# S4 convolution beside a gated FFN on one core: where the second half of the decay exponentials is made

## The chip, the core and the metric

The kernel runs on one core of one Trainium2 chip. The time is device microseconds of one execution, and the median of several executions is quoted. Five engines work side by side: TensorE (PE, with its weight loads PEld), VectorE (DVE), ScalarE (ACT), GpSimd (POOL) and SyncE (SP, which here only issues DMAs).

## The reference, cut to what matters

The reference normalises the input, runs an S4 convolution and a gated FFN on it, adds both to the input, and returns that output with the gradients of twelve inputs. L = 2048 positions, D = 576 channels, N = 128 states per channel, F = 4608.

```python
xn = layernorm(u)
# S4: a long convolution with a kernel K made from the parameters
dt = exp(log_dt)[:, None]
logdA = dt * (A_re + 1j * A_im)                    # [D, N]
P = exp(logdA[:, :, None] * arange(L))             # [D, N, L]
K = einsum("dn,dnl,dn->dl", C, P, dt * B).real     # [D, L]
y = irfft(rfft(pad(xn)) * rfft(pad(K)))[:L] + xn * Dskip
# FFN
gate, up = xn @ W_gate, xn @ W_up
h = relu(gate) * up
out = u + y + h @ W_down
# and the gradients of all of this for a given grad_out
```

The part that the change is about is the real factor of P: exp(dt * A_re * l). It is made at 40 exponents l for each channel and state (16 small steps, 8 steps of 256, 16 steps of 16), and products of these give all 2048.

## The kernel before, in words

Two generators make the program. `Ffn.gen` emits the FFN: 12 chunks of 384 hidden columns; in each chunk four groups of 512 positions go through `a_unit` (three products into PSUM, gating on ACT and DVE) and `outdx` (output and input gradient), and after the last group come the weight gradients (`dw_down`, `dw_gu`, `dw_left`), which are long series of matmuls with few evictions. `S4.gen` emits the convolution in the stages below. Both yield estimated microseconds. The main function advances `S4.gen` by 0.9 units (`PACE`) for each unit that the FFN has yielded. The framework then puts each engine's instructions into one queue per engine, in roughly this order, but ahead of it where it expects an instruction to be ready earlier; the profile shows such moves of some microseconds.

`S4.gen` works on two halves of the channels, 288 each:

- `p1(hf)` transforms the input and the output gradient, multiplies the spectra and makes dk, the gradient of K. It has three sections, with a gap of units ahead of each.
- `params` loads the parameters, makes `pw` (four rows of products per channel), and makes the decay exponentials in 36 steps of 16 channels, named `ex_step`: DVE multiplies `pw` by the 40 exponents into a tile of 128 x 640 fp32, ACT takes Exp in place, and SP stores it to the DRAM tensor `ex_dram` (320 KB). The tile, `exs`, has five rotating buffers (pool `par_ex`).
- `p2(hf)` makes K from the parameters, 16 channels at a time (18 times for a half): it loads a tile `ex` back from `ex_dram` (two buffers, pool `k_ex`), makes angles in `xa` and `W` (one buffer each, pool `k_x`; `W` is two tiles of 128 x 640 side by side; lines L838 to L843), and multiplies. `sums` and `turn` use the result on TensorE. At its end `param_grads` uses `xa` and `W` once more.
- `p3(hf)` transforms K and finishes the convolution of that half.

`both(a, wa, b, wb)` weaves two generators so that their yields stand in the ratio wa to wb. The order is

```python
both(p1(0), 68, params, 45)
both(p2(0), 320, p1(1), 60)
both(p2(1), 320, p3(0), 58)
p3(1)
```

Added up, the yields are 82 units for `p1(0)`, 42 for `params`, 382 for each `p2`, 61 for `p1(1)`, 49 for `p3(0)` and 59 for `p3(1)`. In the last chunk of the FFN, `outdx` takes the results of both `p3` into its sums; whatever is left of `S4.gen` is emitted before that.

DVE and ACT evictions from PSUM are shared out by `Balance.copy`, which keeps a running estimate of the work of both engines and takes the less loaded one.

Of the kernel before, what the change touches and what calls it, by code (L numbers as in the profile page):

```python
# [2 lines left out]

# [7 lines left out]
F32 = mybir.dt.float32  # L11
ACT = mybir.ActivationFunctionType
ALU = mybir.AluOpType
AX = mybir.AxisListType
P = 128
# [5 lines left out]
L, D, F, N = 2048, 576, 4608, 128  # L21
ST = 16
DH = D // 2
# [8 lines left out]
SX = 16  # L32
NE = 40
# [3 lines left out]
W1, W2, W3 = 60.0, 400.0, 58.0  # L37
# [58 lines left out]
def iota(nc, ap, pattern, base, mult):  # L96
    nc.gpsimd.iota(ap, pattern=pattern, base=base, channel_multiplier=mult, allow_small_or_imprecise_dtypes=True)
# [378 lines left out]
class S4:  # L476
# [85 lines left out]
    def params(self, pw):  # L562

        g, nc, bal = self.g, self.g.nc, self.g.bal
        v = nc.vector
        with ExitStack() as c:
            pool = self.pool(c, "par_raw", 1)
            exp_ = self.pool(c, "par_ex", 5)
            raw = pool.tile([P, 6, D], BF16, name="raw")
            nc.sync.dma_start(raw[:], self.par_in[:])  # L570
            ldt = pool.tile([P, D], BF16, name="ldt")
            nc.sync.dma_start(ldt[:], self.log_dt.rearrange("(o d) -> o d", o=1).to_broadcast([P, D]))
            yield 1.0
            dt = pool.tile([P, D], F32, name="dtf")
            nc.scalar.activation(dt[:], ldt[:], ACT.Exp)
            nc.sync.dma_start(self.dt_dram[:], dt[:])
            Ar, Ai, Br, Bi, Cr, Ci = (raw[:, i, :] for i in range(6))
            v.tensor_tensor(pw[:, 0, :], Ar, dt[:], op=ALU.mult)
            bal.add(d=0.7, a=0.7)
            yield 1.0  # L580

            def ex_step(i):
                shp = [P, SX, NE]
                ex = exp_.tile(shp, F32, name="exs")
                v.tensor_tensor(ex[:], pw[:, 0, i * SX:(i + 1) * SX].unsqueeze(2).to_broadcast(shp), self.ev[:].unsqueeze(1).to_broadcast(shp), op=ALU.mult)
                nc.scalar.activation(ex[:], ex[:], ACT.Exp)
                nc.sync.dma_start(self.ex_dram[:, i], ex[:])
                bal.add(d=0.75, a=0.65)

            for i in range(0, 8):  # L590
                ex_step(i)
                yield 1.0
            p1 = pool.tile([P, D], F32, name="p1")
            p2 = pool.tile([P, D], F32, name="p2")
            v.scalar_tensor_tensor(pw[:, 1, :], Ai, 1.0 / TWO_PI, dt[:], op0=ALU.mult, op1=ALU.mult)
            for j, (y1, y2, op) in enumerate(((Br, Bi, ALU.subtract), (Bi, Br, ALU.add))):
                v.tensor_tensor(p1[:], Cr, y1, op=ALU.mult)
                v.tensor_tensor(p2[:], Ci, y2, op=ALU.mult)
                v.tensor_tensor(p1[:], p1[:], p2[:], op=op)
                v.tensor_tensor(pw[:, 2 + j, :], p1[:], dt[:], op=ALU.mult)  # L600
                bal.add(d=2.6)
                yield 2.0
            for i in range(8, D // SX):
                ex_step(i)
                yield 1.0

    def dft(self, pool, dram):

        def load(m):
            S = pool.tile([P, 2, 2, P], BF16, name="Sx")  # L610
            self.g.nc.sync.dma_start(S[:], dram[:, 2 * m:2 * m + 2])
            return S
        return load
# [394 lines left out]
    def gen(self):  # L1008
        g, nc = self.g, self.g.nc
        self.make_dft16()  # L1010
        yield 1.0
        yield from self.make_dft128()
        with ExitStack() as cp:
            kp = self.pool(cp, "s4_par", 1)
            pw = kp.tile([P, 4, D], F32, name="pw")
            self.ev = kp.tile([P, NE], F32, name="ev")
            self.ones = kp.tile([P, 1], F32, name="ones")
            nc.vector.memset(self.ones[:], 1.0)
            iota(nc, self.ev[:, 0:16], [[1, 16]], 0, 0)
            iota(nc, self.ev[:, 16:24], [[256, 8]], 0, 0)  # L1020
            iota(nc, self.ev[:, 24:40], [[16, 16]], 0, 0)
            yield from self.both(self.p1(0, 4, 10.0), 68.0, self.params(pw), 45.0)
            with ExitStack() as c:
                pools = self.p2_pools(c)
                yield from self.both(self.p2(0, pools, pw), 0.8 * W2, self.p1(1, 2, 3.0), W1)
                yield from self.both(self.p2(1, pools, pw), 0.8 * W2, self.p3(0, 2, 3.0), W3)
            yield from self.p3(1, 4, 8.0)

class Final:
# [216 lines left out]
```

## Time and profile before

| | us |
|---|---|
| median of 3 runs | 1824.65 (1823.95 to 1829.02) |
| the profiled execution, its time | 1821.82 |
| its span | 1820.1 |
| TensorE busy | 1732.4 (95%) |
| VectorE busy | 1352.4 (74%) |
| ScalarE busy | 1188.5 (65%) |
| first and last start of an exponential step on DVE | 102.3 and 215.8 |
| first start of L838 in p2(0) | 229.6 |
| first start of L838 in p2(1) | 892.6 |
| last store of p3(1) | about 1609 |

The profile is one execution. A line of it names the line of the kernel, the engine, the operation and its tiles, and in square brackets how long the engine stood idle just before, and who ended that. A busy TensorE is not TensorE at its peak, since matmuls overlap. The granted clock is 1.00 almost everywhere.

### The profile page before, as it was taken

The page shows a single profiled execution, that of the slowest core. Times are in us where ns is not written, and L with a number is a line of the kernel's source. Part 1 is how long each engine was busy: PE and PEld are TensorE (multiplying, and loading weights), DVE is VectorE, ACT ScalarE, POOL GpSimd, SP SyncE. Part 2 cuts the span into 40 slices and gives each one's busy share as a digit, 9 for nine tenths or more (in the row PEclk, how much of TensorE's full clock was granted, in tenths as well). Part 3 has the DMA queues.
Part 4 walks back from the last instruction along what each step waited for, and adds up shares of the span by engine and source line. Part 5 has one row for each costly group of instructions (what it writes and reads, how often), then busy time and mean ns, then how long its engine had stood idle before and what let it go on. Part 6 is the DMA issues. An engine that isn't in the chain of part 4 may idle for free. (4 is left out here: it accounts for less than half of the span.)

```text
span 1820.1 us, 42158 instructions
## 1 busy us (share of the span) xinstructions
PE 1732.4 (95%) x16303; PEld 1182.6 (65%) x16449; DVE 1352.4 (74%) x3175; ACT 1188.5 (65%) x2716; POOL 204.6 (11%) x246
## 2 busy tenths in 40 slices
PE   7998989999999999999999999999999998999998
PEld 5664557667666666766766766766676775466776
DVE  7575885786898788687787888899888865952551
ACT  5875865786588478577478657747857837852551
POOL 0200012111012012102101101101111100010000
PEclk9999999999999999999999999999999999999999
DMA  8789999668557666776866856865665689884883
GB/s 287 261 313 320 304 290 276 191 176 230 178 127 191 197 183 140 238 187 125 238 171 162 227 166 138 206 193 133 166 182 142 133 230 273 252 238 131 264 247 97
DMA packets 239004, 373.30 MB, mean 205 GB/s; under 512 B 49490, under 2 KB 153428, under 8 KB 237268
## 3 DMA queue, kind: packets, MB, share of 16 engines
q1 hardware_dynamic: 212836, 304.09, 51.3%
q0 software_dynamic: 24384, 51.92, 19.1%
q10 hardware_dynamic: 1584, 14.60, 2.2%
q8 instruction: 128, 2.10, 0.5%
q14 instruction: 72, 0.59, 0.1%
HBM read 233.10 MB, written 137.43 MB: 204 GB/s over the span
## 5 line engine op out<-in xcount | busy, mean ns | idle before, releaser
L68 ACT CAST osx<-ps_mm 128x288 bf16<-128x288 f32 x682 | 262.1, 420 | 61.9 <-PE ps_mm L301 59.2
L314 POOL DMA_DIRECT2D acc_dram<-osx x160 | 139.2, 876 | 1016.6 <-ACT osx L68 680.5
L301 PE MATMUL ps_mm<-wf,dgT 128*128 128x288 bf16 x1152 | 207.0, 286 | 8.5 <-ACT osx L68 5.3
L355 PEld LDWEIGHTS <-rows 128*128 128x128 bf16 x1536 | 146.6, 98 | 95.0 <-issue 3.1
L301 PE MATMUL ps_mm<-wf,duT 128*128 128x288 bf16 x1152 | 205.8, 286 | 0.0
L301 PE MATMUL ps_mm<-wf,hT 128*128 128x288 bf16 x1152 | 183.8, 287 | 7.9 <-DVE hT L256 4.3
L244 PE MATMUL ps_mm<-gT,wd_160 128*128 128x512 bf16 x694 | 177.3, 382 | 7.2 <-ACT obd L68 5.3
L244 PE MATMUL ps_mm<-xT,wd_159 128*128 128x512 bf16 x711 | 180.8, 381 | 0.8 <-ACT obw L68 0.3
L244 PE MATMUL ps_mm<-xT,wd_158 128*128 128x512 bf16 x595 | 168.8, 379 | 7.9 <-issue 1.0
L254 DVE SCALAR_TENSOR_TENSOR upm<-rg,ps_mm 128x512 bf16<-128x512 bf16 x144 | 98.2, 682 | 102.0 <-PE ps_mm L244 80.2
L339 PE MATMUL ps_mm<-rows,hN 128*128 128x144 bf16 x2304 | 156.7, 226 | 0.0
L339 PEld LDWEIGHTS <-hN 128*128 128x128 bf16 x2304 | 147.0, 98 | 3.4 <-issue 1.2
L355 PE MATMUL ps_mm<-duN,rows 128*128 128x384 bf16 x768 | 137.9, 326 | 0.0
L355 PE MATMUL ps_mm<-dgN,rows 128*128 128x384 bf16 x768 | 136.9, 327 | 0.0
L68 ACT CAST obw<-ps_mm 128x384 bf16<-128x384 f32 x102 | 48.5, 477 | 133.7 <-PE ps_mm L355 98.9
L301 PEld LDWEIGHTS <-dgT 128*128 128x128 bf16 x1152 | 106.0, 97 | 40.5 <-issue 15.1
L301 PEld LDWEIGHTS <-duT 128*128 128x128 bf16 x1152 | 112.1, 98 | 29.1 <-DVE duT L264 0.2
L301 PEld LDWEIGHTS <-hT 128*128 128x128 bf16 x1152 | 104.5, 98 | 37.1 <-issue 8.2
L68 ACT CAST dhb<-ps_mm 128x512 bf16<-128x512 f32 x141 | 83.8, 594 | 64.5 <-PE ps_mm L244 60.8
L930 DVE TENSOR_REDUCE Sm<-pr 128x8 f32<-128x256 f32 x288 | 119.1, 414 | 3.5
L252 ACT ACTIVATE rg<-ps_mm 128x512 bf16<-128x512 f32 x144 | 87.0, 604 | 51.1 <-PE ps_mm L244 47.4
L244 PEld LDWEIGHTS <-wd_159 128*128 128x128 bf16 x720 | 65.4, 98 | 62.6 <-issue 3.6
(2516 smaller groups left out, 3516.1 us busy)
## 6 DMA issues: line engine op xcount, KB each, us to landing
acc_dram<-osx POOLq DMA_DIRECT2D x176, 288.0 KB, 4.8
gT<-in_gT_dram SPq DMA_DIRECT2D x48, 640.0 KB, 6.4
xT<-xT_dram SPq DMA_DIRECT2D x44, 640.0 KB, 6.0
rows<-in_gq_dram SPq DMA_DIRECT2D x48, 576.0 KB, 4.6
wf<-in_Wf_dram ACTq DMA_DIRECT2D x11, 1296.0 KB, 9.7
ex_dram<-exs SPq DMA_DIRECT2D x36, 320.0 KB, 3.7
ex<-ex_dram SPq DMA_DIRECT2D x36, 320.0 KB, 3.6
out_dram<-obw SPq DMA_DIRECT2D x96, 96.0 KB, 2.7
```

Of the source, the lines that this page charges most:

```text
L68: self.nc.scalar.copy(out, in_)
L244: nc.tensor.matmul(ps[:], lhsT=w[:, k, fs], rhs=rhs[:, k, :], start=(k == 0), stop=(k == NK - 1))
L252: nc.scalar.activation(rg[:], ps_g[:], ACT.Relu)
L254: nc.vector.scalar_tensor_tensor(upm[:], rg[:], 0.0, ps_u[:], op0=ALU.is_gt, op1=ALU.mult)
L301: nc.tensor.matmul(ps[:, cs], lhsT=lt, rhs=rh, start=(i == 0), stop=(i == len(mms) - 1))
L314: nc.gpsimd.dma_start(g.acc_dram[:, t, :, :], o[:], accum_op=ALU.add)
L339: nc.tensor.matmul(ps[:, ft * 144:(ft + 1) * 144], lhsT=self.hN[:, st, ft * P:(ft + 1) * P], rhs=gq[:, st, :], start=(st == 0), stop=(st = ...
L355: nc.tensor.matmul(ps[:, :Fc], lhsT=xs[:, st, 0:P], rhs=src[:, st, :], start=(st == 0), stop=(st == ST - 1))
L930: nc.vector.tensor_reduce(out=Sm[:, vi, s0 + dd:s0 + dd + DG, :], in_=pr[:], op=ALU.add, axis=AX.X)
```

## The change

`params` makes only the 18 exponential steps of the first half of the channels (8 of them before the products of `pw`, 10 after). The other 18 are made by a new generator, `late_ex`, which runs right after `p2(0)` and its `param_grads`, ahead of `p2(1)` and inside the same weave with `p3(0)`. It takes its five buffers from the pools of `p2`: the two halves of `W`, `xa`, and the two `ex` tiles. Each of its steps yields 1.2 units where a step in `params` yielded 1.0. Step, tiles and `ex_dram` keep their shapes. The five buffers `exs` of `params` stay as they are.

```diff
-            for i in range(0, 8):
-                ex_step(i)
+            for i in range(0, 8):
+                self.ex_step(i, exp_.tile([P, SX, NE], F32, name="exs")[:], pw)
                 yield 1.0
...
-            for i in range(8, D // SX):
-                ex_step(i)
+            for i in range(8, DH // SX):
+                self.ex_step(i, exp_.tile([P, SX, NE], F32, name="exs")[:], pw)
                 yield 1.0
+
+    def ex_step(self, i, ex, pw):
+        nc = self.g.nc
+        shp = [P, SX, NE]
+        nc.vector.tensor_tensor(ex, pw[:, 0, i * SX:(i + 1) * SX].unsqueeze(2).to_broadcast(shp), self.ev[:].unsqueeze(1).to_broadcast(shp), op=ALU.mult)
+        nc.scalar.activation(ex, ex, ACT.Exp)
+        nc.sync.dma_start(self.ex_dram[:, i], ex)
+        self.g.bal.add(d=0.75, a=0.65)
+
+    def late_ex(self, pools, pw):
+        exp_, xp = pools[3], pools[4]
+        todo = list(range(DH // SX, D // SX))
+        while todo:
+            W = xp.tile([P, 2, SX, NE], F32, name="W")
+            bufs = [W[:, 0], W[:, 1], xp.tile([P, SX, NE], F32, name="xa")[:]] + [exp_.tile([P, SX, NE], F32, name="ex")[:] for _ in range(2)]
+            for b, i in zip(bufs, todo[:5]):
+                self.ex_step(i, b, pw)
+                yield 1.2
+            todo = todo[5:]
...
-                yield from self.both(self.p2(1, pools, pw), 0.8 * W2, self.p3(0, 2, 3.0), W3)
+                yield from self.both(chain(self.late_ex(pools, pw), self.p2(1, pools, pw)), 0.8 * W2, self.p3(0, 2, 3.0), W3)
```

More of the change, by code (lines that the diff above doesn't have):

```diff
@@ L2 @@
 from contextlib import ExitStack
+from itertools import chain
 import concourse.bass as bass
@@ L580, in params @@
             yield 1.0
[L582 to L588, printed above, removed]
             for i in range(0, 8):
-                ex_step(i)
+                self.ex_step(i, exp_.tile([P, SX, NE], F32, name="exs")[:], pw)
                 yield 1.0
```

## The prediction

> **What bounds the kernel now.** The busy table comes first:
>
> ```profile
> PE 1732.4 (95%) x16303; PEld 1182.6 (65%) x16449; DVE 1352.4 (74%) x3175; ACT 1188.5 (65%) x2716; POOL 204.6 (11%) x246
> ```
>
> TensorE is busy for 1732.4 of 1820.1 us. Its work does not change, so what moves the end is its 88 us of idle time. Next, the stages (columns: length, then busy time and instructions of each engine, granted clock, DMA share, GB/s):
>
> ```profile
> 158.00:230.00 72.00, 68.09 (x493) 37.39 (x497) 61.62 (x162) 57.58 (x142) 4.28 (x5) 1.00 0.94 309
> 230.00:300.00 70.00, 64.80 (x575) 45.30 (x579) 54.16 (x133) 47.28 (x110) 14.55 (x15) 0.98 0.98 286
> 300.00:850.00 550.00, 534.75 (x5310) 367.95 (x5358) 428.85 (x939) 384.19 (x874) 71.71 (x75) 1.00 0.70 186
> 850.00:905.00 55.00, 54.68 (x584) 40.52 (x587) 41.01 (x90) 29.14 (x63) 8.66 (x10) 1.00 0.79 206
> 905.00:1476.00 571.00, 548.60 (x5592) 384.75 (x5637) 490.61 (x1115) 395.49 (x881) 74.21 (x78) 0.99 0.67 171
> ```
>
> From 158 to 230 us, where most exponentials are made, DVE, ACT and the DMA engines are all near full, yet TensorE loses only 72 - 68.1 = 3.9 us. Around 850 to 905, where the change puts half of them, TensorE loses 0.3 us. Third, the exponential tile (durations are min/median/max ns; below, what its engine waited for):
>
> ```profile
> L585 DVE TENSOR_TENSOR exs<-pw,ev x36: 815/819/827, 102.3 to 215.8; 128x640 f32<-128x640 f32 x36
> L586 ACT ACTIVATE exs<-exs x36: 726/739/867, 103.6 to 216.7; 128x640 f32<-128x640 f32 x36
> ...
>   DMA ex_dram<-exs: 14.7, 4
> ...
> DMA to landing us min/median/max: 2.3/3.7/7.0
> ```
>
> DVE stood four times, 14.7 us in all, because a buffer's store had not landed. The timelines of DVE and of TensorE show what that costs TensorE:
>
> ```profile
> 144.77 0.82 DVE L585 TENSOR_TENSOR exs<-pw,ev 128x640 f32<-128x640 f32 x1 [8.06 <-DMA ex_dram<-exs]
> 207.70 0.83 DVE L585 TENSOR_TENSOR exs<-pw,ev 128x640 f32<-128x640 f32 x1 [3.55 <-DMA ex_dram<-exs]
> ```
>
> ```profile
> 146.82 2.25 PE L244 MATMUL ps_mm<-gT,wd_160 128*128 128x512 bf16 x5 [5.28 <-ACT obd L68]
> 209.32 0.31 PE L645 MATMUL ps_s_3202<-b_ug,FM 128*64 128x288 bf16 x2 [1.89 <-DVE s_ug L62]
> ```
>
> The wait of 8.06 us held ACT's exponential, an eviction behind it and then TensorE for 5.28 us. The five matmuls after it took 2.25 us where 1.24 is usual: about 1 us more. The wait of 3.55 us cost 1.89 us, and 0.52 us at 212.2. Counting in the DVE timeline, the 18th step starts at 160.1 us: the first wait belongs to step 14, which stays; the second to step 34, which moves.
>
> [...]
>
> **The change part by part.** Pace first. The conv generator is advanced in units that its yields add up to. From L838's first start, 229.6 us, to its first in half 1, 892.6 us, lie 382 units of p2(0) and 61 of p1(1): 663/443, about 1.5 us a unit; between 160 and 230 it is about 1.4. Params shrinks from 42 units to 24, and 21.6 (18 x 1.2) appear before p2(1). So the first p2 starts 18 x 1.4 = 25 us earlier; the late stage, with 0.18 of p3(0) per unit, lasts 21.6 x 1.18 x 1.4 = 36 us, about 868 to 904; everything behind ends 3.6 units, about 5 us, later.
>
> *Early, removed.* 18 DVE steps x 0.819 = 14.7 us, 18 exponentials x 0.739 = 13.3 us of ACT, 18 stores x 320 KB = 5.9 MB of the window's 22.2 MB, 18 issues on SP (median 0.44 us, 8 us of SP). On TensorE the direct gain is the wait of step 34: 1.89 + 0.52 = 2.4 us.
>
> *Early, given back.* p1(0) is no longer diluted. Per unit of p1 params ran 45/68 = 0.66; the rest of p1(0) after params' 24th unit (24/0.66 = 36 of 82) follows back to back. In the 72 us window the engines did 61.6 + 57.6 = 119.2 us. It shrinks to 47; leave out 18 x 1.56 = 28 and 25 us of FFN work at some 0.37 us per us (9): 82 in 2 x 47 = 87%, against 119.2/144 = 83% before. DMA comes out alike: 22.2 - 5.9 - 1.9 = 14.4 MB in 47 us is 306 GB/s, against 309. So the stage is shorter, not emptier. I book 1 us of gain net: below the 2.4 saved, for the denser rest; bounds -7 (nearly all idle from 158 to 300, 3.9 + 5.2, goes) and +3.
>
> *Late, steps.* The same 14.7 us of DVE and 13.3 of ACT in 36 us, in a stage where both have room (41 and 29 of 55 us) and p2 makes no other demand: nothing on TensorE. If that cover went, DVE's 14.7 us would hold FFN evictions; at the rate above (5.28 of 8.06) up to 9.6. The stores are denser than before: 5.9 MB in 36 us is 164 GB/s on top of the stage's 206, together 370, above the 309 that the early window reached at share 0.94. So DMA is full there, and the chunk's rows, xT, gT and wd loads come later; TensorE lost 3.9/72 = 5% in the early window under such a load, which is 2 us of 36. A part of that is the waits priced next; for late loads alone I book +1 (0 to 4).
>
> *Late, new waits.* A step comes every 1.2 x 1.18 x 1.4 = 2.0 us. W's two halves are one buffer, so a new round waits for the store of the half written four steps before: 8 us. It needs 0.82 + 0.74 + 0.44 + 0.5 (hand-offs, my estimate) + 3.7 = 6.2 us, or 9.5 with the slowest landing: 0 to 1.5 us at three round starts, book 1 in all. The last turn is tighter: p2(1)'s L838 writes xa, which step 18 has just sent off, 2.0 us after it; 6.2 - 2.0 = 4.2 us of wait on DVE, where the kernel before went on at 892.61 at once. Behind it in DVE's queue stand FFN's L254 to L264 and copies, and TensorE waits for these. At 5.28/8.06, rounded down because this is the stage of long dw matmuls, +2 (0 to 5). ex stores wait on SP for an exponential, with rows, xT and gT loads behind them on that queue; these are issued ahead, and their lateness is in the 1 us above. The two ex tiles that p2(1) loads were sent off in step 15 at the latest and are free first.
>
> *Late, tables.* One more Exp stage between Sin stages: two loads x 1.28 = 2.6 us of ACT, book +0.5 (0 to 2.6[...]).
>
> *Shift.* From about 205 to 868 the conv work meets other FFN chunks, 25 us off, later 5 us off. TensorE loses 550 - 534.8 = 15 us in 300-850 and 571 - 548.6 = 22 in 905-1476, in stalls that depend on such meetings. Mean 0, -5 to +7.
>
> *Tail.* The final matmuls start at 1673.6 us, p3(1)'s last stores go out near 1609; 5 us later still leaves some 60. Nothing, whatever the sign.
>
> Sum: -1 + 1 + 1 + 2 + 0.5 = +3.5 us. The profiled execution (span 1820.1, time 1821.8) becomes 1825.3; it lies 2.8 below the median 1824.65, so the forecast is 1828.1.
>
> **Rivals.** *Slower: the wait comes back as the bound.* The late stage falls on FFN's change of chunk, where wd, wf, xT, gT and rows are loaded and the 40-slice DMA row of that stretch has long full parts. Should landings reach 7 us and more with the planned order behind reality, the rounds' starts cost what step 14 did: 5.28 + 1 = 6.3 us on TensorE for 8 us of DVE wait. It decides from landings above 5.5 us, where the 1.8 us of spare is used up. One such stall plus the turn at 5 and the tables at 2.6 gives 14, less the early 1: 1837.6; without the full stall, 1831.3. For it: two of 36 steps paid such waits early at DMA share 0.94, and the late stage asks for more bytes per us. Against: five buffers at a step per 2.0 us, and few evictions among the dw matmuls.
>
> *Faster: the early relief is real.* The congestion of 158-300 goes: -7, the late stage costs 1, 1818.6. For it: three resources near full there. Against: the densities above, and only 2.4 us that trace back to moved steps.
>
> *The change does nothing,* because the planner that writes the queues fills the hole with p1 steps and TensorE never saw it: 1824.65, inside the first case.
>
> **How the numbers follow.** 0.3%, or 5.5 us, is about what a measurement of this kernel can tell from no change. Small net (likeliest, 1828.1, own range 1819.2 to 1830.1): 0.44. Slower, with the bad end of the shift: 0.41. Faster, with its good end: 0.15. The range 1819 to 1841 leaves out about a tenth at each end.
>
> **What would show it.** Right: 18 L585-type steps before 165 us and 18 near 865-905; first L838 near 205, first of half 1 near 904 after some 4 us of DVE waiting for a store; six table loads for four; the stall at 146.8 still there; final matmuls fed in time. Wrong: a TensorE idle above 3 us in 860-910 that traces back to ex_dram (slower rival), or idle in 158-300 down from 9 us to below 4 (faster rival). If neither holds and the time still moves by over 6 us, the shift was mis-sized.

## The result, and the profile after

| | before | after |
|---|---|---|
| median, us | 1824.74 | 1851.49 (1850.27 to 1854.88, 4 runs) |
| profiled execution, time / span, us | 1821.82 / 1820.1 | 1854.88 / 1853.2 |

The ratio of after to before is 1.0145, interval [1.0124, 1.0165]: slower by 26.5 us of 1824.7. The forecast was 1828.1, and its range ended at 1841.

The busy table of the profile page of after:

```profile
PE 1744.3 (94%) x16304; PEld 1185.9 (64%) x16449; DVE 1355.2 (73%) x3174; ACT 1195.3 (65%) x2721; POOL 205.3 (11%) x246
```

The same matmuls are busy 12 us longer in a span that is 33 us longer. The stages of after, in the windows that the prediction used (length; busy time and instructions of PE, PEld, DVE, ACT, POOL; granted clock; DMA share; GB/s):

```profile
158.00:230.00 72.00, 70.06 (x503) 36.38 (x508) 59.52 (x175) 54.12 (x139) 3.44 (x4) 1.00 0.91 288
230.00:300.00 70.00, 59.43 (x462) 40.28 (x467) 51.72 (x108) 43.09 (x101) 15.49 (x16) 0.90 0.79 203
300.00:850.00 550.00, 531.65 (x5331) 367.87 (x5375) 429.30 (x934) 381.89 (x861) 69.51 (x73) 1.00 0.70 187
850.00:905.00 55.00, 47.86 (x439) 34.13 (x441) 36.87 (x78) 34.23 (x76) 11.05 (x12) 0.94 0.76 182
905.00:1476.00 571.00, 538.94 (x5364) 372.94 (x5410) 479.95 (x1096) 387.37 (x856) 69.44 (x72) 0.99 0.67 171
```

From 158 to 230 us TensorE is busy 2 us longer than before, about the gain that the prediction had worked out there. From 230 to 300, where neither kernel makes exponentials, it is busy for 59.4 us where it was 64.8, does 462 matmuls instead of 575, and the clock is 0.90. From 850 to 905 it lost 6.8 us, and 9.7 more behind. In the window 230 to 300 DVE, ACT and the DMA engines are all less busy than before while TensorE idles more, so the early loss is not one of full engines.

The exponential steps of after, in the view of their line on DVE (min/median/max ns; first and last start; indented, what DVE waited for just before them, us and times). The line was L585 before and is L604 here:

```profile
L604 DVE TENSOR_TENSOR exs<-pw,ev x18: 814/821/826, 101.9 to 159.9; 128x640 f32<-128x640 f32 x18
...
L604 DVE TENSOR_TENSOR W<-pw,ev x8: 802/820/826, 889.3 to 921.6; 128x640 f32<-128x640 f32 x8
L604 DVE TENSOR_TENSOR ex<-pw,ev x6: 808/820/826, 796.5 to 845.3; 128x640 f32<-128x640 f32 x6
L604 DVE TENSOR_TENSOR xa<-pw,ev x4: 817/826/827, 886.7 to 923.3; 128x640 f32<-128x640 f32 x4
...
  DMA ex_dram<-W: 18.0, 3
...
  DMA ex_dram<-xa: 8.1, 3
  DMA ex_dram<-ex: 5.7, 2
```

The 18 early steps end at 160 us. The 18 late ones are not the rotation of five buffers that the code writes: the six steps in `ex` start 40 to 90 us ahead of the others, among the last turns of p2(0), because these two tiles came free earlier (`param_grads` still worked in W and xa until 886 us). What is left turns on W and xa alone. In the late stage DVE stood 18.0 + 8.1 + 5.7 = 31.8 us. Its timeline in the late stage (start, us, instructions; in brackets the idle time before and who ended it):

```profile
896.57 0.83 DVE L604 TENSOR_TENSOR xa<-pw,ev 128x640 f32<-128x640 f32 x1 [5.72 <-DMA ex_dram<-xa]
901.10 1.56 DVE L604 TENSOR_TENSOR W<-pw,ev 128x640 f32<-128x640 f32 x2 [3.70 <-DMA ex_dram<-W]
...
912.30 1.56 DVE L604 TENSOR_TENSOR W<-pw,ev 128x640 f32<-128x640 f32 x2 [7.37 <-DMA ex_dram<-W]
920.84 1.56 DVE L604 TENSOR_TENSOR W<-pw,ev 128x640 f32<-128x640 f32 x2 [6.98 <-DMA ex_dram<-W]
```

The stores themselves were slow here. For the 12 that left W and xa from 885 to 930 us, as far as the profile has their landing:

```profile
DMA to landing us min/median/max: 2.7/6.1/9.1
```

Those sent off between 889.8 and 903.6 us took 5.8 to 9.1 us, and the first three waits above end as such a store lands. From 885 to 905 us the DMA share is 0.97: the loads of the FFN's next chunk run beside them.

And what two of these waits did on ACT and on TensorE, from the timelines of these engines:

```profile
921.70 0.74 ACT L605 ACTIVATE W<-W 128x640 f32<-128x640 f32 x1 [5.73 <-DVE W L604]
922.35 0.50 ACT L69 CAST obd<-ps_mm 128x432 bf16<-128x432 f32 x1
```

```profile
898.51 0.88 PE L302 MATMUL ps_mm<-wf,dgT 128*128 128x288 bf16 x3 [3.26 <-ACT osx L69]
922.90 2.29 PE L245 MATMUL ps_mm<-gT,wd_160 128*128 128x512 bf16 x5 [5.60 <-ACT obd L69]
```

This is the chain of step 14 again: a store not landed, DVE waits, ACT's exponential waits for DVE, an eviction stands behind the exponential, TensorE waits for the eviction. The wait of 7.37 us that ended at 912.30 lay beside 168 dw matmuls in a row (902.78 to 914.22) and cost only 0.76 us.

The third place is early, where p2(0) and p1(1) start. TensorE's timeline there:

```profile
243.56 0.66 PE L698 MATMUL ps_s_3734<-bC_3678,Sx 128*128 128x288 bf16 x2 [4.64 <-DMA bC_3678<-C_dk_191]
270.62 0.88 PE L302 MATMUL ps_mm<-wf,dgT 128*128 128x288 bf16 x3 [4.01 <-ACT osx L69]
309.81 0.28 PE L642 MATMUL ps_s_4701<-sig,Sx 128*128 128x288 bf16 x1 [4.06 <-ACT fA_4657 L69]
```

None of the three touches an exponential. The first waits for a load of p1(0)'s last section, the second for an eviction behind a step of p2(0), the third for copies of p1(1) on ACT, which stood 5.78 us until a store of p1(1) had landed (`A_ug_188`, sent off at 300.0 us, beside the load of the FFN's next `wf`).

To see where time goes over the whole run I use one measure of my own: the time elapsed minus the matmul work done. Every weight-load record counts as one matmul at the usual spacing of its form in the trace (216 ns for 128x512, 162.5 for 384 columns, 122.5 for 288, 62.5 for 144, 55.5 for a transpose, and so on; matmuls overlap in it, one of 128x288 alone takes 0.29 us and three in a row 0.53); that makes 1674.2 us in every kernel. The increase over a stretch is time lost by TensorE, whether idle or slowed. A profile is one execution, so differences of 3 us or less are not read.

| us lost in | to 350 | 350 to 800 | 800 to 1000 | 1000 to 1500 | 1500 to 1700 |
|---|---|---|---|---|---|
| before | 58.2 | 27.4 | 10.5 | 32.9 | 20.9 |
| after | 70.1 | 25.5 | 32.1 | 33.8 | 25.0 |

So +11.9 around 240 to 350, +21.6 around the late stage and the change from p2(0) to p2(1), and +4 in p3(1). Between, nothing: from 350 to 800 and from 1000 to 1500 us the two kernels lose the same.

### The profile page after: what moved, and what is told of

Its sections match the earlier page's. It is cut to its first block, busy times and chain, and to the rows that moved or that the text cites. A ratio compares the mean times of both kernels' runs of the same rounds, so it can differ in the third digit from the quotient of the medians.

```text
span 1853.2 us, 42177 instructions
## 1 busy us (share of the span) xinstructions
PE 1744.3 (94%) x16304; PEld 1185.9 (64%) x16449; DVE 1355.2 (73%) x3174; ACT 1195.3 (65%) x2721; POOL 205.3 (11%) x246
## 5 line engine op out<-in xcount | busy, mean ns | idle before, releaser
L302 PE MATMUL ps_mm<-wf,dgT 128*128 128x288 bf16 x1152 | 209.7, 288 | 16.4 <-ACT osx L69 13.4
L302 PE MATMUL ps_mm<-wf,hT 128*128 128x288 bf16 x1152 | 185.8, 287 | 10.5 <-DVE upm L255 7.7
L245 PE MATMUL ps_mm<-gT,wd_160 128*128 128x512 bf16 x695 | 178.3, 383 | 13.2 <-ACT obd L69 11.0
L245 PE MATMUL ps_mm<-xT,wd_159 128*128 128x512 bf16 x712 | 182.5, 380 | 0.7 <-issue 0.4
L245 PE MATMUL ps_mm<-xT,wd_158 128*128 128x512 bf16 x594 | 172.6, 382 | 8.4 <-issue 0.8
L340 PE MATMUL ps_mm<-rows,hN 128*128 128x144 bf16 x2304 | 160.8, 229 | 0.0
L340 PEld LDWEIGHTS <-hN 128*128 128x128 bf16 x2304 | 150.8, 99 | 7.6 <-issue 5.1
L302 PEld LDWEIGHTS <-duT 128*128 128x128 bf16 x1152 | 113.0, 98 | 30.6 <-DVE duT L265 0.9
```

The lines of the kernel that those rows point to most:

```text
L245: nc.tensor.matmul(ps[:], lhsT=w[:, k, fs], rhs=rhs[:, k, :], start=(k == 0), stop=(k == NK - 1))
L302: nc.tensor.matmul(ps[:, cs], lhsT=lt, rhs=rh, start=(i == 0), stop=(i == len(mms) - 1))
L340: nc.tensor.matmul(ps[:, ft * 144:(ft + 1) * 144], lhsT=self.hN[:, st, ft * P:(ft + 1) * P], rhs=gq[:, st, :], start=(st == 0), stop=(st = ...
```

## The experiments

Two theories. **Place**: the convolution and the FFN meet at other points than before, and the points where a stage of the convolution starts (p1 to p2, p2(0) to p2(1), p3) lose time there. **Steps**: the late steps cost it, by their waits, their work or their stores. Differences in us below are ratios times 1824.7, each ratio against runs of before on the same chip. The lost time by stretch:

| us lost in | to 350 | 350 to 800 | 800 to 1000 | 1000 to 1500 | 1500 to 1700 |
|---|---|---|---|---|---|
| e1_pace | 58.7 | 29.5 | 19.1 | 32.4 | 31.5 |
| e2_no_late | 70.1 | 25.7 | 17.7 | 41.9 | 30.0 |
| e3_late_twice | 59.6 | 28.8 | 17.2 | 32.2 | 32.8 |
| e4_no_store | 69.3 | 25.8 | 19.1 | 33.4 | 24.9 |
| e5_own2 | 56.0 | 27.2 | 21.0 | 32.7 | 30.6 |
| e9_spread | 54.6 | 37.2 | 12.2 | 32.3 | 21.8 |
| e10_gap | 62.2 | 29.2 | 17.6 | 33.7 | 33.4 |
| e11_pace_no_store | 54.1 | 28.2 | 17.6 | 33.1 | 32.5 |
| e12_pace_no_late | 55.4 | 28.0 | 13.2 | 32.7 | 20.9 |
| e13_catch | 53.8 | 26.8 | 19.2 | 35.4 | 19.6 |
| e14_zero | 57.1 | 29.1 | 23.9 | 33.1 | 21.0 |
| e15_own_early | 50.2 | 28.1 | 21.1 | 26.9 | 20.6 |

**e1_pace: the places given back.** `params` yields 18 empty units where the steps were.

```diff
+            for i in range(DH // SX, D // SX):
+                yield 1.0
```

> The changed kernel with 18 empty yields of 1.0 at the end of params, so that the order of conv and FFN work up to the end of p2(0) is that of the kernel before, without the 18 moved steps. Two-loss theory (11 to 12 us lost before 350 us because p1(0) and p2(0) come 25 us earlier against the FFN, some 20 us lost from 800 to 960 us in the late stage): the early loss goes, the late one stays, about 1840 us. Rival (the early loss belongs to the late stage's cause, or to the missing steps themselves): it stays at about 1851 us. The convolution ends 18 units later, some 26 us, which still leaves about 30 us before the final matmuls.

1840.1 us, ratio 1.0088 [1.0061, 1.0116]: 10.4 us better than after. All of the early loss is gone, though p1(0) and params hold no more work than in after. What is left, 16.1 us over before, lies at 800 to 1000 and, new, behind 1500.

**e10_gap: the 18 empty units behind params.** p1(0) stays undiluted as in after; from p2(0) on everything has its place in the planned order.

```diff
             yield from self.both(self.p1(0, 4, 10.0), 68.0, self.params(pw), 45.0)
+            for i in range(DH // SX, D // SX):
+                yield 1.0
```

> The changed kernel with the 18 empty yields not inside params but right after p1(0) and params: the p1(0) stage runs undiluted and ends early as in the changed kernel, while p2(0) and p1(1) start where they start in the kernel before. In the changed kernel three stalls make the early loss: 4.6 us at 243.6 us (p1(0)'s last section starts before its load has landed), 4.0 at 270.6 (first turn of p2(0)), 4.1 at 309.8 (start of p1(1)). If the starts of p2(0) and p1(1) against the FFN count, the last two go and at most 5 us more than before are lost at 350 us, about 1840 us in all. If the undiluted p1(0) counts, 10 us or more stay lost at 350 us, 1848 us in all.

1844.95 us, 1.0113 [1.0098, 1.0128]. At 350 us it has lost 4.0 more than before, a third of after's 11.9. The stall at 309.8 us is gone; one of 4.09 us at 242.0 and one of 3.64 us at 269.9 stay, the second against the expectation, and the time lies between the two forecasts. The second and third turn of p2(0) still start 14.7 and 12.6 us earlier than before, drawn forward by the framework's planner; from the fourth on they have their place. So about 8 us belong to the earlier places of p2(0) and p1(1), and about 4 to the denser p1(0) together with those two turns, which this run does not part.

**e6_shift18, e7_shift9, e8_later9: the shift alone.** Before, with each of the 36 steps yielding 0.5, 0.75 or 1.25 instead of 1.0. No work moves to another stage; the convolution behind runs 18 or 9 units ahead, or 9 late.

```diff
-                yield 1.0
+                yield 0.5    # 0.75 in e7_shift9, 1.25 in e8_later9
```

> The kernel before with 36 steps in params as they are, but each yields 0.5 units where it yielded 1.0: nothing is moved, the convolution runs 18 units ahead, as in the changed kernel before 800 us. If the meeting of p1(0)'s end, p2(0)'s start and the FFN's change of chunk makes the early loss: 8 to 14 us more lost than before at 350 us, and 1832 to 1850 us in all. If the missing dilution or the missing steps make it: within 4 us of before.

> The same with 0.75 units a step, so 9 units ahead, some 13 us. If what counts is which FFN work meets a stage's start, and not how far the shift goes, the time is not halfway between before and e6_shift18: anything from 1822 to 1848 us, with other stalls. If the loss grows with the shift, about half that of e6_shift18.

> The kernel before with 1.25 units for each step in params where it was 1.0: nothing is moved, the convolution runs 9 units, some 13 us, behind. e7_shift9, 9 units ahead, lost 30 us. If early starts are what costs (stages begun before the FFN's loads are out of the way), later ones cost nothing: 1820 to 1828 us. If any departure from the place at which the kernel before stands costs: 1832 us or more.

1866.57 us, 1.0231 [1.0201, 1.0261]; 1853.71 us, 1.0161 [1.0137, 1.0186]; 1839.61 us, 1.0087 [1.0072, 1.0102]. That is +42, +29 and +16 us for nothing but another place (in e6 and e7 also for denser steps: e6 lost 6 us more by 150 us already). e6 and e7 are slower than anything that was expected of them. Both directions cost. By the measure above, e6 and e7 lose about 22 and 14 us more than before up to 350 us, and 7 to 10 more in each of the three stretches behind 800 us; e8 loses about 6 more up to 350 us, 4 in p2 and 11 behind 1500. One thing moves along with the place: `Balance.copy` hands out evictions by a running count, so another order can also send an eviction to the other engine. No run holds that split fixed.

**e2_no_late: after without its late stage.**

```diff
-            nc.sync.dma_start(ex[:], self.ex_dram[:, hf * (DH // SX) + i])
+            nc.sync.dma_start(ex[:], self.ex_dram[:, i])
...
-                yield from self.both(chain(self.late_ex(pools, pw), self.p2(1, pools, pw)), 0.8 * W2, self.p3(0, 2, 3.0), W3)
+                yield from self.both(self.p2(1, pools, pw), 0.8 * W2, self.p3(0, 2, 3.0), W3)
```

> The changed kernel without late_ex: the second half's exponentials are not made at all, and p2(1) loads those of the first half. Only the early part of the change is left. Two-loss theory: about 1824.7 + 11.5 = 1836 us, with the lost time of TensorE at 350 us as in the changed kernel. Rival (the late stage makes the whole loss): at or a little below 1825 us.

1853.28 us, 1.0158 [1.0139, 1.0176]: a miss. Without any late work the kernel is as slow as after. It has the same early loss, and then, 18 units ahead to the end, 7 us more than before at 800 to 1000, 9 from 1000 to 1500 and 9 behind 1500. In after the late stage's own units cancel this.

**e12_pace_no_late: both.** e1_pace without the late stage.

> e1_pace without late_ex: the second half's exponentials are not made at all and p2(1) loads those of the first half; the empty yields keep the conv in its places from first to last. This is the most that taking the 18 steps out of params can bring: 2.4 us by the stalls that trace back to moved steps, so 1819 to 1824 us. If it were 1816 us or less, the early relief was booked too low; if over 1827 us, the order matters even where the yields do not.

1819.75 us, 0.9980 [0.9972, 0.9988]: all that can be won by taking the 18 steps out is 3.6 us. Against e2_no_late it is only the 18 empty units: 32 us. The starts of the 36 turns of p2 (L838 of before) show what the empty units keep. Minus is earlier than before, in us on the clock:

| turn of p2 | 2 | 6 | 10 | 14 | 18 | 19 | 23 | 27 | 31 | 36 |
|---|---|---|---|---|---|---|---|---|---|---|
| after | -13.2 | -2.2 | -12.3 | -10.8 | -12.1 | 35.4 | 55.3 | 44.1 | 31.5 | 39.8 |
| e1_pace | -3.6 | 1.1 | 1.1 | 2.6 | 2.6 | 26.5 | 49.5 | 45.4 | 35.5 | 37.3 |
| e12_pace_no_late | -4.5 | -3.5 | -3.5 | -2.0 | -2.1 | -2.3 | 0.5 | 0.4 | 0.4 | 0.4 |
| e13_catch | -4.8 | -5.1 | -5.1 | -5.1 | -5.1 | 18.2 | 41.5 | 27.3 | 16.4 | 5.3 |
| e14_zero | -5.2 | -0.9 | -0.9 | 0.6 | 0.6 | 20.8 | 26.3 | 14.5 | 14.5 | 14.4 |
| e15_own_early | -6.9 | -16.0 | -27.8 | -40.3 | -38.6 | -26.3 | 18.7 | 8.4 | -3.2 | -2.7 |

With the empty units p2 runs at an almost constant distance from before, so the same work should meet. In after, where the FFN is itself some 12 us behind from 350 us on, the distance changes from turn to turn, and in the second half (turns 19 to 36) it does so in e1_pace too.

**e3_late_twice: the early steps back as well.** `params` makes all 36 steps, and 18 are made once more late.

```diff
-            for i in range(8, DH // SX):
+            for i in range(8, D // SX):
```

> The changed kernel with params as in the kernel before, so all 36 steps are made early, and late_ex makes the 18 of the second half once more. Only the late part of the change is left. Two-loss theory: about 1824.7 + 20 = 1845 us, nothing lost before 800 us. Rival (the shift makes the whole loss): about 1827 us. The convolution ends 21.6 units later than before, some 31 us.

1837.52 us, 1.0071 [1.0056, 1.0086], between the two forecasts. With e1_pace it agrees within the intervals: 18 real steps in `params`, or 18 empty units, make no difference that is seen; the late stage costs about 13 to 20 us on top of either (e3 against before, e1_pace against e12_pace_no_late).

**e4_no_store: the late steps store nothing.** As in e2_no_late, p2(1) loads the first half's exponentials.

```diff
-        nc.sync.dma_start(self.ex_dram[:, i], ex)
+        if i < DH // SX:
+            nc.sync.dma_start(self.ex_dram[:, i], ex)
```

> The changed kernel with late_ex making its 18 multiplications and Exps but not storing them; p2(1) loads the first half's exponentials. No step waits for a store to land. If the late loss is the wait for the landing (18.0 us on W, 8.1 on xa, 5.7 on the ex tiles, in the trace of the changed kernel): it goes but for 2 to 4 us, 1832 to 1835 us in all, and late_ex's first to last step on DVE is over in 20 us or less. Rival (the late loss is the DVE and ACT work of the steps and the table loads, 14.7 + 13.3 + 3.8 us, in FFN's way): it stays, 1848 to 1852 us.

1841.37 us, 1.0075 [1.0049, 1.0101], against after's 1.0145: 12.8 us, and between the two forecasts. DVE's late waits fell from 31.8 to 2.8 us, and the loss at 800 to 1000 from 32.1 to 19.1. So the stores and the waits for them cost TensorE about 13 us in after, give or take some 6 by the intervals. The 19.1 that remains is about what e2_no_late loses there with no late stage at all, though at another place.

**e11_pace_no_store: the same in e1_pace.**

> e1_pace without the late steps' stores; p2(1) loads the first half's exponentials. Everything else, the order against the FFN included, is that of e1_pace (1840.1). If waits for landings make the late loss, the 8 to 9 us lost from 800 to 1000 us beyond the kernel before fall to 2 or 3, 1833 us in all. If it is the place that p2(1) and p3(0) come to, 25 us behind the kernel before: they stay, 1838 to 1841 us.

1835.74 us, 1.0062 [1.0047, 1.0077]: between the two forecasts, only 4.7 us better than e1_pace, and the two intervals overlap. In e1_pace DVE waits 13.7 us for late stores, not 31.8: the same 18 steps with the same buffers wait less than half as long where they meet another piece of the FFN. There the stores out of W and xa (895 to 930 us) land sooner:

```profile
DMA to landing us min/median/max: 2.2/3.0/4.8
```

The loss behind 1500 stays.

**e5_own2: tiles of their own.** e1_pace, the late steps in two new tiles `lx` and the two `ex`.

```diff
...
-            W = xp.tile([P, 2, SX, NE], F32, name="W")
-            bufs = [W[:, 0], W[:, 1], xp.tile([P, SX, NE], F32, name="xa")[:]] + [exp_.tile([P, SX, NE], F32, name="ex")[:] for _ in range(2)]
...
+            bufs = [lp.tile([P, SX, NE], F32, name="lx")[:] for _ in range(2)] + [exp_.tile([P, SX, NE], F32, name="ex")[:] for _ in range(2)]
```

> Empty yields in params as in e1_pace; late_ex takes two tiles of its own and the two ex tiles, and neither W nor xa, so its steps need not wait for param_grads and no store holds the tile that p2(1) starts with. If the borrowed W and xa are what makes late waits, DVE waits for stores in the late steps come to under 6 us in all (13.7 in e1_pace), and the time is 4 to 8 us below e1_pace (1840.1). If it is the load on the DMA engines, whatever the buffers are, the waits stay above 10 us and the time within 3 us of e1_pace.

1838.86 us, 1.0077 [1.0058, 1.0095]: half a miss. The waits fell to 5.5 us, the time did not follow. In a kernel that keeps its early places, the shared W and xa are worth about 2 us, less than the intervals can tell from nothing.

**e9_spread: three steps in W and xa after every third turn of p2(0),** no late stage, places kept by 18 empty units.

```diff
...
+                n = (s0 + x0) // SX
+                if hf == 0 and n % 3 == 0:
+                    Wb = xp.tile([P, 2, SX, NE], F32, name="W")
+                    xb = xp.tile([P, SX, NE], F32, name="xa")
+                    for b, i in zip((Wb[:, 0], Wb[:, 1], xb[:]), range(DH // SX + n, DH // SX + n + 3)):
+                        self.ex_step(i, b, pw)
...
```

> No late stage. Each third of the 18 turns of p2(0) makes three of the second half's exponentials in W's halves and in xa, just after the turn has done with them, some 25 us ahead of the next use; params has the empty yields, and these steps yield nothing, so the conv keeps its places against the FFN. 12 table loads more on ACT, 15 us over some 600. If the changed kernel's loss is waits for landings plus the moved order, neither is left: 1821 to 1829 us. If 14.7 us of DVE and 28 us of ACT cannot be hidden in p2(0): 1832 us or more, lost evenly between 300 and 800 us.

1831.4 us, 1.0034 [1.0023, 1.0045], just under the second forecast. No loss at 800 to 1000 or behind 1500, but 37.2 us between 350 and 800, where e12_pace_no_late loses 28.0: six interruptions of p2(0), with 12 table loads more than before has, cost about 9 us.

**e13_catch, e14_zero, e15_own_early: the places behind the late stage given back.** With the early places kept, the late stage still costs 20 us (e1_pace against e12_pace_no_late), of which about 5 are waits. The three take away the 21.6 units by which it puts off p2(1), p3(0) and p3(1): e13_catch turn by turn in p2(1), e14_zero at once, e15_own_early by drawing p2(0) forward, with the tiles of e5_own2.

```diff
-                yield 6.0
+                yield 6.0 - 1.2 * hf          # e13_catch, from e1_pace
+                yield 6.0 - 1.2 * (1 - hf)    # e15_own_early, from e5_own2
...
-                yield 1.2
+                yield 0.0                     # e14_zero, from e1_pace
```

> The 18 empty units of the pacing run, and the first yield of each 16 channels in half 1 of kernel generation is 4.8 instead of 6.0 units, so that these 18 turns take back the 21.6 units of the late stage: p3(1) comes at the place it has in the kernel before, p2(1) approaches it turn by turn. The pacing run takes 1840.1 us, and 10 of its 20 us over the pacing run without a late stage are lost after 1500 us. Theory place (p3(1) loses because it meets other FFN work 30 us later): that part goes, about 1830. Theory steps (the late stage itself costs it): 1838 to 1841, and the wait of over 6 us at the start of p3(1) is still there.

> The 18 empty units of the pacing run, and the late steps yield 0 instead of 1.2 units: all 18 stand at one point of the planned order, and p2(1), p3(0) and p3(1) have the places of the kernel before. Theory place: only the waits for stores are left (denser than in the pacing run, 13.7 us of DVE there, up to 30 here) and the time is 1824 to 1830. Theory steps: 1838 or more, since the steps are bunched.

> The run with tiles of their own for the late steps (two lx and two ex, 18 empty units in params), and the first yield of each 16 channels in half 0 is 4.8 instead of 6.0 units: p2(0) ends 21.6 units earlier, the late stage lies ahead of the place where p2(1) starts in the kernel before, and everything after it has its place of before. Theory place: nothing left but p2(0) drawn forward turn by turn, 1822 to 1829. Theory steps: 1836 to 1840 as with the own tiles alone (1838.9).

e13_catch: 1828.39 us, 1.0037 [1.0024, 1.0051], 9.3 us better than e1_pace, with the late stage untouched. Windows of 1500 to 1700 us, first of e1_pace, then of e13_catch:

```profile
1500.00:1700.00 200.00, 184.59 (x1407) 111.50 (x1420) 121.29 (x349) 112.77 (x282) 13.83 (x16) 0.98 0.75 218
```

```profile
1500.00:1700.00 200.00, 192.04 (x1481) 117.96 (x1480) 112.95 (x325) 115.12 (x292) 13.82 (x16) 1.00 0.78 229
```

TensorE does 60 matmuls more in the same time. That is the count of weight loads, 1480 against 1420; the matmul column says 74, but 147 of the 16449 matmul records are missing from the profile of e1_pace and none from that of e13_catch. In e1_pace one line of its timeline says where p3(1) lost most; e13_catch has no stall above 2 us from 1480 to 1670:

```profile
1549.58 0.40 PE L644 MATMUL ps_s<-kk,Sx 128*128 128x288 bf16 x1 [6.55 <-DMA kk<-k_dram]
```

The five kernels in which p3(1) is 21.6 units late beside an otherwise kept order (e1, e3, e5, e10, e11) lose 30.6 to 33.4 us behind 1500; before and the five in which it has its place (e9, e12, e13, e14, e15) lose 19.6 to 21.8.

e14_zero: 1832.68 us, 1.0051 [1.0030, 1.0071], between both expectations. The tail is cured, p2(1) runs 14.4 us behind before at a constant distance from its sixth turn on, and that distance is lost at 800 to 1050, where all 18 steps are bunched. The late steps wait 6.0 us there on W, 5.7 on xa and 2.3 on `ex`; one more line of the list of waits (us, times, longest) is the turn from the late stage to p2(1):

```profile
DVE W L855 <- DMA ex_dram<-W: 3.9, 1, 3.9
```

The prediction had priced this turn at 4.2 us of DVE.

e15_own_early: 1824.09 us, 1.0004 [0.9995, 1.0013]: as fast as before, 13.3 us better than e5_own2, from which it differs only in 18 yields. So here the late stage costs about what taking the steps out of `params` saves, 4 us. No version run here that does all the work is faster than before. Its profiled execution took 1818.66 us, 5.4 less than its median, so its row of lost time is not read to a few us.

## Why the prediction was wrong

Undone in this order, the parts add up: 10.4 us for the early place (after to e1_pace), 9.3 for the place of what follows the late stage (e1_pace to e13_catch), 10.4 for the late stage itself, with p3(1) alone back in its place (e13_catch to e12_pace_no_late), less the 3.6 us that taking the steps out of `params` brings. The split depends on the order: the waits for stores are worth 12.8 us in after and 4.7 in e1_pace.

**Shift: the step that failed first.** It was booked at mean 0, -5 to +7, because TensorE's losses in p2 "depend on such meetings" and could go either way. p2(0) hardly loses by it: 25.5 to 29.5 us from 350 to 800 in every kernel of the tables but e9_spread. The losses lie mostly where stages begin (e2_no_late, e6 and e7 lose 7 to 10 us in the middle of p2(1) as well), and no shift alone brought a gain: +16, +29 and +42 us in e8, e7 and e6, +29 in e2_no_late, 32 between e2_no_late and e12_pace_no_late. The prediction looked for the cost where the shifted time lies and not where the stages begin. Its last sentence kept a mis-sized shift for the case in which no mark holds; here a mark holds and the shift was mis-sized too. In the sum above the term measures about +10 early and +9 behind the late stage; of the 10 some 4 are what e10_gap leaves, in part the denser p1(0), which the prediction had under Early. That not every other place is bad is seen in e15_own_early, whose p2(1) starts 26 us earlier than before, in a kernel that is as fast; what a given place costs was not foreseen from the profile of before, and no rule for it came out of the runs.

**Early.** Gain and give-back were booked at -1, with bounds -7 and +3. The gain alone, with the places kept and p1(0) diluted by empty units, is 3.6 us where 2.4 was worked out. That p1(0), undiluted, is "shorter, not emptier" was right in kind; it costs up to 4 us (e10_gap) where 1.4 was booked. Together that is about nothing in place of -1, inside the bounds. The pace argument had p2(0) start 25 us earlier. On the clock it was 13 for the second turn and 2 to 16 after that; the first turn alone was drawn to 164.6 us, by the framework's planner, in e1_pace and e12_pace_no_late as well.

**Late, steps: work at nothing.** Not contradicted by any single line, but not shown. With places or buffers mended, e13_catch still loses 6 us more at 800 to 1000 than e12_pace_no_late, e5_own2 and e15_own_early 8, e11_pace_no_store 4. Whether that is the 28 us of DVE and ACT work, the table loads (two more than before in e13_catch and e5_own2, four in e15_own_early), or the turn to p2(1) itself stays open; the stalls in e15_own_early are short ones (1.44, 1.55, 2.75 and 1.17 us), none at a store.

**Late, new waits: booked +3 in all, about 13 in after.** Two of its inputs failed. The first is "a step comes every 2.0 us" over five buffers: it took the written order for the order run. `ex` was free early, so its six steps went ahead, and the twelve others shared W and xa, with rounds of W 8.5 to 11.8 us apart (889.3, 901.1, 912.3, 920.8). The second is the landing, taken as 3.7 us, the median of the early window. Over all 36 steps it stayed near that (median 3.5), but in the late stage it was 6.1 us, up to 9.1. The prediction had said that the DMA is full there and had laid this on the loads alone, not on the stores that the rounds wait for. e1_pace has the same tiles and the same early `ex`, a median landing of 3.0 us, and 13.7 us of waits. DVE waited 31.8 us where some 5 were allowed for; no run parts the two causes further. The slower rival, which named landings above 5.5 us as its condition, then came true: the mark "TensorE idle above 3 us in 860 to 910 that traces back to ex_dram" is met at 898.5 us (3.26), and a larger one lies just behind at 922.9 (5.60). The rival's price of a wait (5.28 of 8.06 us) suits: 13 of 31.8 is less, since some fell under dw matmuls, as the prediction argued. Its total, 1837.6, left out the shift. The 0.5 us for hand-offs was my estimate, from no stated number; in before, the exponential at 108.61 us starts 0.04 us after the end of its step on DVE (107.75 + 0.82).

**The turn (xa), booked +2.** DVE waited 1.35 us on xa there in after, and 3.9 to 4.0 on W in e1_pace, e13_catch and e14_zero, close to the 4.2 worked out for xa. No TensorE cost was isolated.

**Late loads, booked +1.** TensorE's stalls from 890 to 930 trace to evictions, not to rows, xT, gT or wd; so for the loads alone the term was of the right size or too high. What landed late there, at a DMA share of 0.97 from 885 to 905 us, were the stores, with a median of 6.1 us.

**Tables, booked +0.5 for two loads.** There are eight loads instead of four, not six, since the first hoisted `ex` step stands between two Sins (e1_pace, where it does not, has six):

```profile
L605 ACT ACT_TABLE_LOAD x2 | 2.6, 1283 | 0.0
...
L855 ACT ACT_TABLE_LOAD x3 | 3.8, 1283 | 0.1
```

The Sin of this line loaded once before. A load takes 1283 ns in before too (L841). Four more loads are 5.1 us of ACT, twice the 2.6 worked out, and no run prices them alone; e9_spread, with twelve more, bounds these and its interruptions together at about 9 us, and e15_own_early, with eight as well, is as fast as before.

**Tail, booked at nothing because 60 us are spare.** Spare it had, for the final matmuls. But p3(1) can lose time at its own start, 6.55 us on `kk` in e1_pace; the sum had no term for that.

**The other marks.** The stall at 146.8 us is still there (5.43 us at 146.64). The first L838 was to start near 205 us and starts at 164.6. The late steps were to run from 865 to 905 us; six run from 796 to 846 and twelve from 887 to 924. Half 1's first turn was to start near 904 us and starts at 928.0.

## What to carry to other kernels

When work is moved inside one of two interleaved streams, everything behind it in that stream moves too: price that first, above all at the starts of stages. It takes one run to measure, with empty units left in the place of the work. Count a rotation of buffers by which of them come free first, since a planner that hoists ready steps turns five buffers into three; take a store's landing time from the place to which the work goes (6.1 us here), not from where it came (3.7); and follow every wait down the engines' queues to the eviction that stands behind it (8.06 us of DVE's wait became 5.28 on TensorE in before).

## What the runs showed of the hardware

*DVE beside GpSimd.* The stall at 270.6 us in after starts with slow DVE operations. From the timeline of 255 to 273 us:

```profile
264.76 1.68 POOL L843 TENSOR_TENSOR dkc<-dkr,lv 128x512 bf16<-128x512 bf16 x1
...
265.00 1.52 DVE L864 TENSOR_SCALAR A_4452<-A_4451 128x256 bf16<-128x256 bf16 x1
...
266.39 1.03 POOL L842 COPY dkc<-dkr 128x512 bf16<-128x512 bf16 x1
266.44 1.52 DVE L867 TENSOR_TENSOR B<-W,ex 128x512 bf16<-128x512 f32 x1
267.38 1.91 POOL L843 TENSOR_TENSOR dkc<-dkr,lv 128x512 bf16<-128x512 bf16 x1
267.89 1.94 DVE L869 TENSOR_TENSOR X<-W,ex 128x512 f32<-128x512 f32 x1
```

L864, L867 and L869 take 0.22, 0.69 and 0.68 us where POOL is not at L842 or L843. In the whole of after the 7 that overlap these POOL lines take 1.19 to 1.94 us, and none of the 101 others is above 0.7. What holds the DVE operations up in that time was not shown. A plan that takes the usual 0.22 us for L864 is 1.3 us off at 1.52, and behind the three in a row ACT stood 4.30 us before its own X (L870, 269.87 us), with TensorE's evictions queued behind that.

*The clock behind a stall.* Windows of 10 us in after that hold two of the long stalls:

```profile
240.00:250.00 10.00, 6.45 (x31) 4.23 (x32) 4.02 (x10) 2.33 (x6) 0.00 (x0) 0.66 0.82 246
920.00:930.00 10.00, 7.10 (x27) 3.30 (x27) 6.15 (x10) 4.17 (x8) 0.00 (x0) 0.66 0.68 254
```

The granted clock is 0.66 in these and 1.00 in the 10 us on either side of them. Taken finer, it is 0.50 from 242.5 to 248.5 and from 922 to 928 us, and behind the stall at 270.6 from 270 to 276. Each of these stretches begins in the last 1.5 us of its stall (4.64 us, ended at 243.56; 5.60, at 922.90; 4.01, at 270.62). It followed shorter stalls as well. Behind the one of 2.75 us that ended at 868.52 us in e15_own_early:

```profile
870.00:872.00 2.00, 2.00 (x14) 1.44 (x13) 0.00 (x0) 1.12 (x3) 0.00 (x0) 0.50 1.01 403
```

In before, 2.07 us of idle that ended at 1255.74 were followed by 0.50 from 1256.5 to 1259.5, but 2.50 us that ended at 1510.11 by 1.00, so no threshold comes out of these traces, and what sets the clock was not shown. Summed over 230 to 330 us, 1 minus the clock makes 8.5 us in after and 1.7 before, and part of it fell on idle time. So TensorE lost more there than the length of the stalls: behind the one of 5.60 us the five matmuls at 922.90 took 2.29 us where 1.24 is usual.
